# Attention with squared ReLU, then a token and channel mixer, on one Trainium2 core: a change to the planner that orders all its work

## The chip, the cores and the metric

The kernel runs on one core of one Trainium2 chip. TensorE (PE in the profile) multiplies matrices, VectorE (DVE) and ScalarE (ACT) empty its PSUM banks and do the elementwise work, GpSimd (POOL) issues the loads, and SyncE (SP) issues transposes by DMA and the stores. The metric is the device time of one execution in microseconds (us); lower is better.

## The reference

Eight batches, twelve heads, 448 positions, 64 elements a head. The attention has no softmax: the scores go through ReLU, are squared and divided by the length. Its output is the input of a mixer: one pair of products along the positions (tokens), one along the 768 channels.

```python
scores = scale * np.matmul(q, k.transpose(0, 1, 3, 2))
attn = np.maximum(scores, 0.0) ** 2 / S
x = np.matmul(attn, v)                      # then (B, S, H * D)
h = np.maximum(x.T @ w_tok1, 0.0) @ w_tok2  # 448 -> 256 -> 448, per batch
u = x + h.T
h2 = np.maximum(u @ w_ch1, 0.0) @ w_ch2     # 768 -> 1536 -> 768
out = u + h2
```

## The kernel before

The work is cut into 24 steps of four heads (three steps a batch). All products are in bf16. The names below are those of the planner's operations.

A step `s` begins with the loads of its k, q and v, issued by POOL in a fixed order (`ld`, line 386), into one of four buffers each. For k and q the head dimension must come onto the partitions. Up to step 7 this is done on PE (`T`, line 518), and ACT and DVE copy the result from PSUM (`cp`). From step 8 on it is done by DMA: DVE copies k, then q, into the tile `side` (`ik`, `iq`, line 592), and SP issues a DMA transpose from `side` into the tile `kqT` (`xk`, `xq`, line 599). There is one `side` tile, with a half for k and a half for q, so a copy of step s has to wait for the transpose of step s-1:

```python
Op(f"i{t}{s}", "DVE", emit, loads[s, t] + [cross.get((s - 1, t))], durs={"DVE": 0.534}, slack=9.0, rank=IRANK)
```

The scores come in seven chunks a step (`S`, lines 628 and 648, tiles of 64x64 rows and columns of PE, four at a time). Each chunk fills two PSUM banks; ACT or DVE apply the ReLU into a buffer `sq` (lines 363 and 365), DVE squares it (line 690). There are 13 such buffers. The product with v (`V`, lines 712 and 739) takes the seven chunks; ACT and DVE bring its two banks into the tile `xT` (`xe`).

Then the tokens are mixed: `xT` is transposed on PE (`X`, line 827) or, from step 9 on, by a DMA on SP (`xd`, line 806); `t1` and `t2` (lines 857 and 887) are the two products, and DVE adds their result to x (`u`, line 901) into the tile `uT_sb`. Of that tile SP makes a transposed copy by DMA (`ub`, line 927), which only the last addition of the kernel needs.

The channels are mixed once a batch (three steps) is there: 12 units `C1` of six matmuls (line 949, needing the weight tile `wc1`), and for each 128 rows two units `C2` of 12 matmuls (line 1022, needing the weight tile `wc2`). Each unit fills a PSUM bank. The evictions of C2 (`c2e`, line 1038) are on DVE; they add the transposed copy of u and so wait for `ub`. The stores go out through SP. `wc1` is loaded in two halves and `wc2` in three thirds, between the loads of the steps.

All of this is ordered when the kernel is built, by a class `Planner`. It walks through the time in steps of 0.01 us with a planned duration for each operation, picks the next operation for each engine, and writes the instructions in that order. On the chip each engine and each queue then works through its list in order, waiting on semaphores, whatever the planned times were. How long a DMA is planned to take follows from constants: its `work`, the share of the engines that it gets while both queues are busy (`SHARE`), a time behind it (`POST`) and a safety margin (`LATE`, `QLATE` for `kqT`, `XLATE` for `xd`, `ULATE` for `ub`). A larger margin puts the users of the data further back in the order; it does not hold anything on the chip.

Two more things stand in the kernel before. `hold`: the `ub` transposes of the first `HOLD` = 1 step get a wait for the last half of `wc1`, and since SP works in order the ones behind them wait too. And idle matmuls (`fill`, line 1100): where PE has had nothing to do for over 0.1 us of planned time, between 4.55 and 16 us, the planner writes small products of a zero tile whose result nobody reads.

Of the kernel before, what the change touches and what calls it, by code (L numbers as in the profile page):

```python
# [9 lines left out]
FP32 = mybir.dt.float32  # L10
BF16 = mybir.dt.bfloat16
# [10 lines left out]
FRONT, LOOKP, LOOKV = 40.0, 0.0, 0.0  # L22
# [16 lines left out]
class Op:  # L39
    def __init__(self, name, eng, emit, deps=(), **kw):  # L40
        self.name, self.eng, self.emit = name, eng, emit
        self.deps = [d for d in deps if d is not None]
        self.on = None
        self.start = self.seen = None
        self.banks = 0
        self.bank = []
        self.frees = None
        self.rank = 0
        self.shape = None
        self.work = None  # L50
        self.durs = None
        self.late = None
        self.drain = self.adds = 0.0
        self.slack = 0.3
        self.away = 100
        self.__dict__.update(kw)

    def ready(self, t):
        return self.left == 0 and self.at <= t


class Planner:
# [10 lines left out]
    def done(self, o):  # L73
        for d in o.users:
            d.left -= 1
            d.at = max(d.at, o.seen)
            if d.left == 0:
                self.open[d.pool].append(d)

    def moved(self, t, step):  # L80
        heads = [q for q in self.rings.values() if q and q[0][0] <= t]
        share = SHARE_W if heads and heads[0][0][2].name[:2] == "wc" else SHARE
        for q in heads:
            q[0][1] -= step * (1.0 if len(heads) == 1 else share if q[0][2].eng == "SP" else 1.0 - share)
            if q[0][1] <= 0:
                _, _, o = q.pop(0)
                o.seen = t + POST[o.eng]
                self.landed[o.eng].append(o.seen)
                o.seen += LATE[o.eng] if o.late is None else o.late
                self.done(o)  # L90

    def run(self, stream, gap, enter, tol, lanes=8):
# [28 lines left out]
        while left:  # L121
# [23 lines left out]
            for e in ("ACT", "DVE"):  # L145
# [13 lines left out]
                o = best[1]  # L159
                if t < FRONT and o.rank >= 2 and any(  # L160
                    u.rank <= 1 and u.eng == e and u.at < t + LOOKV * o.durs[e] for u in self.open["FLEX"]
                ):
                    continue
                self.open["FLEX"].remove(o)
# [11 lines left out]
            if free["PE"] <= t:  # L176
# [5 lines left out]

                def urgent(u):
                    return u.rank <= 1 if u.shape == "m" else u.name[:2] in ("V0", "V1", "V2")

                pick = None
# [10 lines left out]
                ends = late and sc.head and pick is not None  # L197
                if late and va is not None and va.first is None and va.step > (vstep if shape == "s" and sc.head else sc.vstep):
                    va = None
# [22 lines left out]
                else:  # L222
# [16 lines left out]
                    else:  # L239
                        o = pick  # L240
                if t < FRONT and LOOKP and o is not None and not urgent(o):
                    soon = [u for u in self.open["UNIT"] if u.rank <= 1] + ([va] if va is not None and urgent(va) else [])
                    soon = [u for u in soon if u.left == 0 and sum(b <= u.at for b in banks) >= u.banks]
                    now = [u for u in soon if fits(u)]
                    if now:
                        o = min(now, key=lambda u: (u.rank, u.n))
                    elif any(u.at < t + LOOKP * o.dur for u in soon):
                        o = None
# [44 lines left out]
def kernel(  # L293
# [47 lines left out]
    kqT = [[t[:, h] for t in kqTs] for h in range(2)]  # L341
    side = sbuf.tile([128, 2, KC, 128], BF16, name="side")
    q_first = side.rearrange("p a c d -> p (a c d)").bitcast(FP32).rearrange("p (e n) -> p e n", e=2)
    v_first = sbuf.tile([128, 4, 4 * D], BF16, name="v_first")
    sqs = [sbuf.tile([128, 2, S], BF16, name=f"sq{i}") for i in range(NSQ)]
# [241 lines left out]
    def crossing(s):  # L587
        for j, t in enumerate("kq"):

            def emit(o, j=j, t=t):  # L590
                src = raws[t][s % NR].rearrange("p e (c d) -> p c e d", c=KC)
                nc.vector.tensor_copy(side[:, j].rearrange("p c (e d) -> p c e d", e=2), src)

            i = raw_last[s, t] = add(
                Op(f"i{t}{s}", "DVE", emit, loads[s, t] + [cross.get((s - 1, t))], durs={"DVE": 0.534}, slack=9.0, rank=IRANK)
            )

            def emit(o, j=j):
                nc.sync.dma_start_transpose(
                    out=kqTs[s % NQ][:, j].rearrange("p (c n) -> p c n", c=KC),  # L600
                    in_=side[:, j].rearrange("p c n -> p (c n)"),
                )
# [18 lines left out]
    def score(s, c):  # L621
# [61 lines left out]
        if (s, c) == (1, SPLIT):  # L683
# [9 lines left out]
                slack=9.0,  # L693
                rank=2.1,
            )
# [3 lines left out]
    def value(s):  # L699
# [50 lines left out]
        for cs in parts:  # L750
# [13 lines left out]
            if s == 0:  # L764
                firsts.append(u)
            vals.update({s * KC + c: u for c in cs})
        raw_last[s, "v"] = u
# [28 lines left out]
    def mixing(s):  # L796
# [124 lines left out]

        hold = [wc1_ops[EC - 1]] if s < HOLD else []
        for a in range(2):
# [68 lines left out]
    def channel2(bb, t):  # L992
# [22 lines left out]
        for i, (g0, g1) in enumerate(parts):  # L1015
            cols = slice(g0 * 128, g1 * 128)
            size = (g1 - g0) * 128

            def emit(o, cols=cols, size=size):
                o.ps = bank(o, 0, "m2_ps")  # L1020
                for e in range(EC):
                    nc.tensor.matmul(  # L1022
# [119 lines left out]
```

## Time and profile before

| | |
|---|---|
| median of 3 runs | 367.15 us (364.5, 367.15, 369.16) |
| the profiled execution | 362.89 us, of which the span is 361.1 us |
| PE busy | 353.0 us (98%) |
| DVE busy | 247.7 us (69%) |
| ACT busy | 187.7 us (52%) |
| DMA packets | 98313, 50.32 MB |
| DMA transposes | 48 of `uT_sb`, 32 of `side`, 15 of `xT` |

The span runs from the first to the last instruction; the execution's own time has 1.8 us around it. A busy PE is not a PE at its peak: matmuls are pipelined and a record's length covers the pipe, so the pace is read from the starts of consecutive ones. The profiled execution is below all three runs.

### The profile page before, as it was taken

How to read it: one execution, taken by the hardware profiler on the slowest of the kernel's cores; microseconds unless marked ns; L12 is line 12 of the kernel's file. 1: busy time of each engine (PE TensorE's matmuls, PEld its weight loads, DVE VectorE, ACT ScalarE, POOL GpSimd, SP SyncE). 2: the span in 40 equal slices, each digit the busy share in tenths (PEclk: the TensorE clock that was granted, in tenths of full speed). 3: DMA queues.
4: the chain of work that ended last, by engine and by line, in shares of the span. 5: the costliest groups of instructions: out<-in, count | busy, mean ns of one | idle time of the engine just before them, and what ended most of it. 6: DMA issues, size and time to landing. Idle time of an engine off the chain costs nothing.

```text
span 361.1 us, 8783 instructions
## 1 busy us (share of the span) xinstructions
PE 353.0 (98%) x3487; PEld 200.1 (55%) x3487; DVE 247.7 (69%) x464; ACT 187.7 (52%) x388; POOL 91.1 (25%) x156
## 2 busy tenths in 40 slices
PE   8899999999899999999999999999999999999995
PEld 4556546555455554565555665556555665555564
DVE  3999598957699775998699978748699832011032
ACT  4999576637688256643674543652487212413300
POOL 8944414713323131233033321301000000000000
PEclk9999999999999999999999999999999999999999
DMA  8999999999989999999999999996621554011044
GB/s 146 187 206 200 181 183 172 190 158 204 120 122 183 213 157 147 184 120 195 185 113 145 183 147 227 140 167 120 152 40 33 95 116 120 13 45 44 0 109 112
DMA packets 98313, 50.32 MB, mean 139 GB/s; under 512 B 71968, under 2 KB 94816, under 8 KB 98272
## 3 DMA queue, kind: packets, MB, share of 16 engines
q1 hardware_dynamic: 73504, 28.16, 45.0%
q0 software_dynamic: 24608, 21.51, 44.5%
q8 instruction: 27, 0.44, 0.5%
q10 hardware_dynamic: 160, 0.10, 0.1%
q14 instruction: 14, 0.11, 0.1%
HBM read 43.45 MB, written 11.01 MB: 151 GB/s over the span
## 4 chain that ended last, share of the span: by engine, by line
PE 81%; DMA 6%; ACT 4%; issue 4%; DVE 2%; POOL 1%; ACTq 0%; POOLq 0%; DVEq 0%
PE m_ps L1022 28%; PE m_ps L949 26%; PE sc_ps L648 7%; PE acc_ps L739 7%; PE t_ps L857 5%; DMA q_raw<-in_q_dram 5%; PE h_ps L887 4%; ACT sq L363 3%; DMA k_raw<-in_k_dram 2%; DVE sq L690 1%; PE warm_ps L448 1%; DVE sq L365 1%; PE x_ps L827 1%; PE kqT_ps L518 1%; ACT kqT L369 1%
## 5 line engine op out<-in xcount | busy, mean ns | idle before, releaser
L363 ACT ACTIVATE sq<-sc_ps 128x448 bf16<-128x448 f32 x226 | 109.2, 583 | 38.6 <-PE sc_ps L648 37.8
L949 PE MATMUL m_ps<-uT_sb,wc 128*128 128x448 bf16 x576 | 115.4, 353 | 0.1
L1022 PE MATMUL m_ps<-wc,r_sb 128*128 128x384 bf16 (+2 forms) x684 | 114.1, 323 | 0.0
L690 DVE TENSOR_TENSOR sq<-sq 128x896 bf16<-128x896 bf16 x168 | 96.8, 616 | 1.0
L1022 PEld LDWEIGHTS <-r_sb 128*128 128x128 bf16 x684 | 65.8, 98 | 44.4 <-issue 2.7
L363 ACT ACTIVATE r_sb<-m_ps 128x448 bf16<-128x448 f32 x96 | 52.3, 546 | 68.0 <-PE m_ps L949 67.6
L949 PEld LDWEIGHTS <-wc 128*128 128x128 bf16 x576 | 55.2, 98 | 52.1 <-issue 4.1
L365 DVE TENSOR_SCALAR sq<-sc_ps 128x448 bf16<-128x448 f32 x110 | 63.5, 615 | 22.1 <-PE sc_ps L648 21.5
L1038 DVE TENSOR_TENSOR out_sb<-m_ps,u_sb 128x384 f32<-128x384 f32 (+2 forms) x57 | 31.2, 548 | 68.7 <-PE m_ps L1022 68.6
L386 POOL DMA_DIRECT2D v_raw<-in_v_dram x46 | 27.7, 615 | 127.9 <-PE sc_ps L648 89.0
L648 PE MATMUL sc_ps<-kqT 64*64 64x448 bf16 x644 | 50.2, 356 | 2.5 <-DVE sq L365 1.6
L739 PE MATMUL acc_ps<-sq,v_raw 64*64 64x448 bf16 x644 | 40.1, 350 | 0.0
L386 POOL DMA_DIRECT2D k_raw<-in_k_dram x48 | 29.2, 622 | 16.7 <-DMA wc<-in_moe_w_ch_dram 8.7
L363 ACT ACTIVATE r_sb<-t_ps 128x512 bf16<-128x512 f32 (+1 forms) x27 | 16.0, 604 | 29.3 <-PE t_ps L857 29.3
L648 PEld LDWEIGHTS <-kqT 64*64 64x64 bf16 x644 | 18.6, 105 | 22.0 <-issue 14.8
L901 DVE TENSOR_TENSOR uT_sb<-h_ps,xT 128x448 bf16<-128x448 f32 x48 | 28.0, 615 | 2.8 <-PE h_ps L887 2.8
L386 POOL DMA_DIRECT2D q_raw<-in_q_dram x46 | 28.1, 631 | 4.2 <-DVE out_sb L1038 1.6
L857 PE MATMUL t_ps<-x_sb,wt 128*128 128x256 bf16 (+1 forms) x216 | 25.1, 261 | 0.0
L739 PEld LDWEIGHTS <-v_raw 64*64 64x64 bf16 x644 | 18.8, 107 | 11.2 <-issue 1.6
L887 PE MATMUL h_ps<-wt,r_sb 128*128 128x448 bf16 x96 | 23.0, 354 | 0.1
L857 PEld LDWEIGHTS <-wt 128*128 128x128 bf16 x216 | 18.3, 98 | 7.0 <-issue 3.9
L772 ACT ACTIVATE xT<-acc_ps 128x448 bf16<-128x448 f32 x24 | 13.8, 573 | 12.6 <-PE acc_ps L739 12.5
(39 smaller groups left out, 118.3 us busy)
## 6 DMA issues: line engine op xcount, KB each, us to landing
out_dram<-out_sb SPq DMA_DIRECT2D x54, 192.0 KB, 3.0
k_raw<-in_k_dram POOLq DMA_DIRECT2D x48, 112.0 KB, 5.7
q_raw<-in_q_dram POOLq DMA_DIRECT2D x46, 112.0 KB, 6.9
v_raw<-in_v_dram POOLq DMA_DIRECT2D x46, 112.0 KB, 4.6
wc<-in_moe_w_ch_dram POOLq DMA_DIRECT2D x2, 1152.0 KB, 12.9
wc<-in_moe_w_ch_dram POOLq DMA_DIRECT2D x3, 768.0 KB, 14.7
u_sb<-uT_sb SPq DMA_TRANSPOSE x48, 5.4
kqT<-side SPq DMA_TRANSPOSE x32, 6.3
```

Source lines behind the costliest of these rows:

```text
L363: o.ins = nc.scalar.activation(out, ps, AF.Relu)
L365: o.ins = nc.vector.tensor_scalar(out=out, in0=ps, scalar1=0.0, scalar2=None, op0=ALU.max)
L386: nc.gpsimd.dma_start(out=raws[t][s % NR][64 * half : 64 * (half + 1)], in_=src[b, h0 : h0 + 2].rearrange("e (p c) d -> p e (c d)", c=KC),)
L648: nc.tensor.matmul(o.ps[e][64 * half : 64 * (half + 1), :S], lhsT=lhsT, rhs=rhs, start=True, stop=True, skip_group_check=True,)
L690: lambda o: nc.vector.tensor_tensor(out=buf, in0=buf, in1=buf, op=ALU.mult),
L739: nc.tensor.matmul(o.ps[half][64 * e : 64 * (e + 1), :S], lhsT=r[rows, e, c * D : (c + 1) * D], rhs=sq[rows, e, :], start=(c == 0), stop=( ...
L857: nc.tensor.matmul(o.ps[:, j, :], lhsT=wt1[:, c, j * 128 : (j + 1) * 128], rhs=x_sb[:, p0:p1, c, :], start=(c == 0), stop=(c == 3),)
L887: nc.tensor.matmul(o.ps[:, :S], lhsT=r1[:, j, a * 128 : (a + 1) * 128], rhs=wt2[:, j, :], start=(j == 0), stop=(j == JC - 1),)
L901: nc.vector.tensor_tensor(out=uTs[bb % 2][:, 2 * i + a, off : off + S].rearrange("n (c p) -> n c p", c=KC), in0=t2.ps[:, :S].rearrange("n ...
L949: nc.tensor.matmul(ps[:, :S], lhsT=wc1[:, g, e * 128 : (e + 1) * 128], rhs=uT[:, g, off : off + S], start=(g == 0), stop=(g == CC - 1),)
L1022: nc.tensor.matmul(o.ps[:, :size], lhsT=r2[:, e, t * 128 : (t + 1) * 128], rhs=wc2[:, e, cols], start=(e == 0), stop=(e == EC - 1),)
L1038: nc.vector.tensor_tensor(out=out_sb[:, cols].rearrange("n (g d) -> n g d", d=128), in0=u.ps[:, :size].rearrange("n (g d) -> n g d", d=128 ...
```

## The change

The planner's constants for DMAs change, and two are new: `SPEED` = 0.88 lets all transfers progress more slowly in the planned time, and `REST` = 2.0 puts the DVE copies into `side` 2 us (planned) behind their loads. The margins of `kqT` and `xd` transposes shrink, that of `ub` grows.

There are two `side` tiles, used in turn, and a copy of step s waits for the transpose of step s-2. (The tile that takes the first v is now a view of the second one.)

A score chunk is not placed on PE until the product with v that frees its `sq` buffer has been placed. Evictions and squares of older steps go first (`AGE`).

The first three `C2` units are divided: eight matmuls that need the first two thirds of `wc2`, and four that need the last.

`HOLD` becomes 4, and the wait is for the last third of `wc2` instead of the last half of `wc1`.

Idle matmuls are written at once wherever PE has nothing ready from 4.55 to 11 us of planned time, with a planned duration of 0.08 us before 8 us. There are 53 instead of 43.

A part of the planner that its constants had switched off is removed (left out below).

```diff
-GAP, ENTER, TOL, TPOS = 6.0, 0.5, 0.1, 3
+GAP, ENTER, TOL, TPOS = 6.0, 0.5, 0.15, 3
-QLATE, XLATE, ULATE = 4.0, 6.0, 0.5
-SHARE, SHARE_W = 0.35, 0.11
+REST, SPEED = 2.0, 0.88
+QLATE, XLATE, ULATE = 2.0, 3.0, 3.0
+SHARE, SHARE_W = 0.35, 0.2
-EARLY, PARTIAL = 3, 3
-LATE = {"POOL": 1.5, "SP": 1.0}
+DENSE, COLD = (4.55, 11.0), 8.0
+EARLY, PARTIAL, PARTIAL2 = 3, 3, 3
+LATE = {"POOL": 0.7, "SP": 1.0}
-HOLD = 1
+HOLD = 4
+AGE = 0.03
-ONE, GAP1, WAIT1, NEED1, VSOON, IRANK = 12, 12.0, 0.3, 5, 0.8, 2.0
-STOCK, SLOPE, FGAP = 10.0, 0.4, 0.5
+ONE, GAP1, WAIT1, NEED1, VSOON, IRANK = 12, 12.0, 0.2, 5, 0.8, 2.0
+STOCK, SLOPE, FGAP = 8.0, 0.5, 0.8
...
     def ready(self, t):
-        return self.left == 0 and self.at <= t
+        return self.left == 0 and self.at <= t and (self.old is None or self.old.start is not None)
...
             if d.left == 0:
+                d.at += d.rest
                 self.open[d.pool].append(d)
...
     def moved(self, t, step):
+        step = step * SPEED
...
-                if o is None and 4.55 < t < FILL and idle > 0.1:
+                quiet = o is None and DENSE[0] < t < FILL and (t < DENSE[1] or idle > 0.1)
+                if quiet:
...
-                        d = 0.056
+                        d = 0.08 if t < COLD else 0.056
...
-    side = sbuf.tile([128, 2, KC, 128], BF16, name="side")
+    sides = [sbuf.tile([128, 2, KC, 128], BF16, name=f"side{i}") for i in range(2)]
...
-                Op(f"i{t}{s}", "DVE", emit, loads[s, t] + [cross.get((s - 1, t))], durs={"DVE": 0.534}, slack=9.0, rank=IRANK)
+                Op(f"i{t}{s}", "DVE", emit, loads[s, t] + [cross.get((s - 2, t))], durs={"DVE": 0.534}, slack=9.0, rank=IRANK, rest=REST)
...
         sc[s, c] = u
+        u.old = vals.get(s * KC + c - NSQ)
...
-                    rank=2.05 if (s, c) != (1, SPLIT) else 1,
+                    rank=(2.05 if (s, c) != (1, SPLIT) else 2.0) + AGE * min(s, 4),
...
-        hold = [wc1_ops[EC - 1]] if s < HOLD else []
+        hold = [wc2_ops[EC - 1]] if s < HOLD else []
...
-            deps = [c1e[2 * bb + h, e] for h in range(2) if (t <= HT if h == 0 else t >= HT) for e in range(EC)]
-            deps += list(wc2_ops.values())
-            u = Op(f"C2.{bb}.{t}.{i}", "PE", emit, deps, shape="m", banks=1, dur=12 * (size / 2400 + 0.0025), rank=2)
+            def needs(es):
+                hs = [h for h in range(2) if (t <= HT if h == 0 else t >= HT)]
+                return [c1e[2 * bb + h, e] for h in hs for e in es] + [wc2_ops[e] for e in es]
+
+            if n * 2 + i < PARTIAL2:
+                es = range(2 * EC // 3)
+                first = Op(f"C2.{bb}.{t}.{i}a", "PE", lambda o, es=es, emit=emit: emit(o, es), needs(es), shape="m", banks=1, dur=len(es) * one, rank=2)
...
+                es = range(2 * EC // 3, EC)
+                u = Op(
+                    f"C2.{bb}.{t}.{i}",
+                    "PE",
+                    lambda o, es=es, first=first, emit=emit: emit(o, es, first),
+                    needs(es) + [first],
...
+            else:
+                es = range(EC)
+                u = Op(f"C2.{bb}.{t}.{i}", "PE", lambda o, es=es, emit=emit: emit(o, es), needs(es), shape="m", banks=1, dur=EC * one, rank=2)
```

More of the change, by code (lines that the diff above doesn't have):

```diff
@@ L197, in run @@
                 ends = late and sc.head and pick is not None
-                if late and va is not None and va.first is None and va.step > (vstep if shape == "s" and sc.head else sc.vstep):
+                stuck = sc is not None and sc.old is not None and sc.old.start is None
+                if late and not stuck and va is not None and va.first is None and va.step > (vstep if shape == "s" and sc.head else sc.vstep):
                     va = None
@@ L240, in run @@
                         o = pick
[L241 to L248, printed above, removed]
-                if o is None and 4.55 < t < FILL and idle > 0.1:
+                quiet = o is None and DENSE[0] < t < FILL and (t < DENSE[1] or idle > 0.1)
+                if quiet:
                     if filling is None:
@@ L600, in emit @@
                     out=kqTs[s % NQ][:, j].rearrange("p (c n) -> p c n", c=KC),
[L601 removed]
+                    in_=sides[s % 2][:, j].rearrange("p c n -> p (c n)"),
                 )
@@ L693, in score @@
                 slack=9.0,
-                rank=2.1,
+                rank=2.1 + AGE * min(s, 4),
             )
@@ L765, in value @@
                 firsts.append(u)
-            vals.update({s * KC + c: u for c in cs})
+            vals.update({s * KC + c: u for c in (cs if s else range(KC))})
         raw_last[s, "v"] = u
@@ L1017, in channel2, with emit @@
             size = (g1 - g0) * 128
-            def emit(o, cols=cols, size=size):
-                o.ps = bank(o, 0, "m2_ps")
-                for e in range(EC):
+            def emit(o, es, first=None, cols=cols, size=size):
+                if first is None:
+                    o.ps = bank(o, 0, "m2_ps")
+                else:
+                    o.ps, o.bank = first.ps, first.bank
+                for e in es:
                     nc.tensor.matmul(
```

24 lines of the change are left out of this document (13 added, 11 removed).

## The prediction

> **What bounds the kernel now.** I read the page first, then busy time by stages of 10 us, then the timelines of PE and DVE where a stage shows a gap. The page:
>
> ```profile
> span 361.1 us, 8783 instructions
> PE 353.0 (98%) x3487; PEld 200.1 (55%) x3487; DVE 247.7 (69%) x464; ACT 187.7 (52%) x388; POOL 91.1 (25%) x156
> DMA  8999999999989999999999999996621554011044
> ```
>
> PE is busy 98% of the span, and the DMA engines are full until about 260 us. By stages (PE first, then PEld, DVE, ACT, POOL, each with its count):
>
> ```profile
> 0.00:10.00 10.00, 8.49 (x108) 4.77 (x108) 4.13 (x13) 5.31 (x10) 8.88 (x20) 1.00 0.89 149
> 10.00:20.00 10.00, 8.93 (x211) 5.43 (x207) 9.90 (x19) 9.96 (x22) 9.31 (x16) 1.00 1.25 190
> 20.00:30.00 10.00, 9.88 (x188) 6.55 (x190) 9.87 (x20) 10.00 (x26) 4.45 (x8) 1.00 1.20 206
> ...
> 90.00:100.00 10.00, 8.37 (x82) 4.35 (x81) 6.53 (x13) 6.75 (x15) 3.56 (x6) 1.00 1.25 125
> ...
> 350.00:360.00 10.00, 7.41 (x58) 4.96 (x56) 2.57 (x6) 0.00 (x0) 0.00 (x0) 1.00 0.47 119
> sum 360.00, PE 352.96 PEld 200.07 DVE 247.68 ACT 187.70 POOL 91.14; mean PE 9.80 PEld 5.56 DVE 6.88 ACT 5.21 POOL 2.53
> ```
>
> Of 360 us PE is idle 7.04: 2.70 before 30 us, 1.63 between 90 and 100, 2.59 behind the last product, and 0.12 elsewhere. So this kernel is bound by PE from 30 us on; before that by ACT and DVE, which are both full from 10 to 30 us. In this execution, then, a better order has one hole to win, and something at the start. Here is the hole, on PE and on DVE:
>
> ```profile
> 95.33 0.54 PE L648 MATMUL sc_ps<-kqT 64*64 64x448 bf16 x5
> 97.50 0.38 PE L648 MATMUL sc_ps<-kqT 64*64 64x448 bf16 x3 [1.63 <-DVE sq L365]
> 97.81 1.31 PE L949 MATMUL m_ps<-uT_sb,wc 128*128 128x448 bf16 x6
> ```
>
> ```profile
> 91.24 1.68 DVE L690 TENSOR_TENSOR sq<-sq 128x896 bf16<-128x896 bf16 x3
> 96.30 0.62 DVE L592 COPY side<-k_raw 128x896 bf16<-128x896 bf16 x1 [3.37 <-DMA q_raw<-in_q_dram]
> 96.83 0.61 DVE L365 TENSOR_SCALAR sq<-sc_ps 128x448 bf16<-128x448 f32 x1
> ```
>
> DVE stands still for 3.37 us in front of the copy of k into `side`; the eviction behind it (L365) is what PE waits for. The profile names a load of q, but a copy of k reads no q. By the code it waits for its own k and for the DMA transpose of the step before, which reads the one `side` tile that the copy overwrites. That transpose:
>
> ```profile
> L599 SPq DMA_TRANSPOSE kqT<-side x1: 2440/2440/2440, 84.1 to 84.1; - x1
> DMA to landing us min/median/max: 12.0/12.0/12.0
> ```
>
> 84.1 + 12.0 = 96.1, and the copy starts at 96.30. So I take the reuse of `side` as the cause.
>
> Other runs of this kernel took 364.5, 367.15 and 369.16 us; the profiled one took 362.89 (span 361.1 and 1.8 around it). 1.6 to 6.3 us are lost in runs that no trace shows. What the trace shows is how little lies between some landings and their use:
>
> ```profile
> L386 POOL DMA_DIRECT2D q_raw<-in_q_dram x1: 600/600/600, 42.6 to 42.6; - x1
> DMA to landing us min/median/max: 18.3/18.3/18.3
> ...
> L435 POOL DMA_DIRECT2D wc<-in_moe_w_ch_dram x1: 760/760/760, 38.8 to 38.8; - x1
> DMA to landing us min/median/max: 18.0/18.0/18.0
> ...
> L386 POOL DMA_DIRECT2D q_raw<-in_q_dram x1: 590/590/590, 58.5 to 58.5; - x1
> DMA to landing us min/median/max: 6.4/6.4/6.4
> ```
>
> ```profile
> 60.00 1.52 PE L739 MATMUL acc_ps<-sq,v_raw 64*64 64x448 bf16 x28
> 61.35 0.39 PE L518 MATMUL kqT_ps<-ident,k_raw 64*64 64x64 bf16 x28
> ...
> 65.84 0.41 PE L518 MATMUL kqT_ps<-ident,k_raw 64*64 64x64 bf16 x28
> ...
> 57.71 0.31 PE sc_ps L648 x4
> 58.02 2.06 PE m_ps L1022 x12
> ```
>
> The q of step 6 lands at 60.9 and its transposes (T6) start at 61.35: 0.5 us in hand. The last third of `wc2` lands at 56.8 and C2.0.0.0 starts at 58.02: 1.2 us. The q of step 7 lands at 64.9 for T7 at 65.84: 0.9 us. Where transfers take a tenth longer, each of the first two is 1.8 us later and PE, which takes its work in order, waits.
>
> **The change part by part.** The work on PE stays: the same products, the same 118 changes between 64x64 and 128x128 tiles in both orders, the divided products have their 12 matmuls as 8 and 4. The prices that I move work with, from the chain that ended last:
>
> ```profile
> 295.36 5.85 PE m_ps L1022 x36
> 301.21 0.87 PE t_ps L857 x8
> ...
> 303.98 13.62 PE m_ps L949 x72
> ```
>
> So a C2 unit (12 matmuls) is 5.85/3 = 1.95 us, a C1 unit (6) is 13.62/12 = 1.14, a t1 0.87.
>
> *Two side tiles.* The k copy now waits for the transpose of two steps before. The 2.0 us go: without the wait the C1 at 97.81 would start about 95.8, one score's 0.4 behind 95.33. DVE's other waits of this kind,
>
> ```profile
> DVE side L592 <- DMA kqT<-side: 3.0, 2, 1.7
> ```
>
> held no matmul, and are worth nothing on PE. Bounds 1.6 (the gap shown) to 2.1; I take 2.0.
>
> *Longer transfers in the plan* (SPEED, REST, QLATE, XLATE, LATE). This only moves work. In the changed order, T6 has two thirds of C2.0.0.1 and t1.4.0 more in front, and V5 (60.00 to 61.35) and S5.6 (0.31) less: 1.30 + 0.87 - 1.35 - 0.31 = half a us more in hand. T7 has 5 C2 and 9 C1 units more in front: 9.8 + 10.3 us. Up to V8 (the products with v of step 8), 14 C2 units are done instead of 6, so step 8 comes 15.6 us later against its loads. Worth 0 in an execution without lateness; in the others up to the 4.3 us between the profiled execution and the median. Price if it fails: the margin taken off the x transposes (XLATE 6 to 3) leaves t1 waiting, about a us each for the few that now land closest. I take 0 for the profiled execution.
>
> *Divided C2.* C2.0.0.0 starts with 8 matmuls that need two thirds of `wc2`; the last third is needed 1.30 + 0.87 us later (t1.4.0 stands between), so its margin grows from 1.2 to about 3 us. 0 us in the profiled execution.
>
> *Late channel-input transposes.* The eight transposes of steps 0 to 3 now wait for the last third of `wc2`, and the four of steps 4 and 5 stand behind them on SP's queue. Before, the two of step 0 waited for the last half of `wc1`, and eleven went from 29.80 on:
>
> ```profile
> 29.80 39.93 SPq L927 DMA_TRANSPOSE u_sb<-uT_sb  x11
> ...
> L927 SPq DMA_TRANSPOSE u_sb<-uT_sb x2: 1711/2598/3484, 45.7 to 49.3; - x2
> DMA to landing us min/median/max: 14.5/15.2/15.8
> ...
> L927 SPq DMA_TRANSPOSE u_sb<-uT_sb x3: 1189/1220/1464, 65.3 to 68.5; - x3
> DMA to landing us min/median/max: 6.4/6.5/9.8
> ```
>
> Behind them on SP stand the transposes of step 8 and the stores. Waiting for them: the evictions of C2 on DVE, behind those the u additions of step 5 and the copies into `side`; and six C2 units keep six of eight PSUM banks until then. Counting rows from C2.0.0.0a at 57.7, the sixth C2 unit ends near 76, and with two banks for t2.5 PE stops there if the third transpose has not landed. At 1.22 us an issue it is issued by 56.8 + 2 x 1.22 = 59.2 and lands between 65.7 (6.5 later) and 75.0 (15.8 later). Cost 0 at that pace, with 1 us in hand at the worst; the gain is on the loads from 30 to 57 us, which held no matmul here. I take 0.
>
> [...]
>
> *Idle matmuls.* 53 instead of 43, in the first step:
>
> ```profile
> 4.58 0.63 PE L1100 MATMUL fill_ps<-warm 128*128 128x128 bf16 x4
> ...
> 6.25 0.94 PE L1100 MATMUL fill_ps<-warm 128*128 128x128 bf16 x10
> ...
> 11.46 0.84 PE L1100 MATMUL fill_ps<-warm 128*128 128x128 bf16 x12
> ```
>
> Ten more are 10 x 0.07 to 10 x 0.16 us of PE, in stretches where PE has nothing ready and ACT and DVE set the pace (up to V0 both engines have the same number of instructions in both orders). The four at 4.58 take twice the time each of the twelve at 11.46, so early work on PE is slow; denser work might end that sooner. Bounds: 1.6 lost to 1.1 won (half of the 2.2 us from 4.58 to 6.8). I take 0.
>
> *Sum.* 362.89 - 2.0 = 360.9 us for an execution like the profiled one. For the median of runs I add nothing for lateness, since each margin of under 1.2 us found here grows; bounds 0 to 4.3. Forecast 361.0, 6 us under the median of before.
>
> **The rivals.**
> *Faster still, near 359.3.* Early PE work gets to full speed sooner (1.1) and 0.5 of the 2.70 us that PE idles before 30 us goes: 360.9 - 1.6. For it: the slow idle matmuls. Against it: ACT and DVE are full from 10 to 30 us. [...]
> *The lost time of the other runs is not lateness.* Then 4.3 us stay on top: 360.9 + 4.3 = 365.2. For it: all three runs lie above the profiled one. Against it: margins of 0.5 to 1.2 us behind landings of 18 us.
> *Slower, 370.* SP issues the held transposes at the 3.5 us that one took at 45 to 49 us, and they land after 15.8: the sixth is issued at 56.8 + 5 x 3.5 = 74.3 and lands at 90; the second group of C2 evictions, in front of the squares of step 6 on DVE, is due near 81 (76 and four C1 units): 9 us of PE, 361 + 9 = 370. It decides from 6 us on; with a second such round (the loads of steps 7 to 9 pushed back) over 374.5. Against it: landings behind the weights took 6.4 to 9.8.
>
> **How the numbers follow.** Forecast 361.0 (own range 359.8 to 363): 0.40. Faster, 359.3: 0.32. Lost time stays: 0.12. Slower: 0.16, of which 0.04 within 2%. 2% of 367.15 is 7.3 us, about what a measurement of this kernel can tell from no change; under 359.8 is faster, over 374.5 slower. So faster 0.32, within 2% 0.56, slower 0.12. The range 358.3 to 368.0 leaves out most of the slower rival and a little below.
>
> **What would show it.** Right: no gap on PE at the k copies, T7 over 15 us behind its loads, a span near 359.2, idle of PE under 0.5 us from 30 to 350. Wrong: a PE gap between 70 and 95 us ended by an output eviction or a u addition on DVE; t1 waiting for x transposes; idle matmuls followed by a later V0 than before.

## The result and the profile after

The changed kernel takes 360.81 us (median of 6 runs, 360.34 to 360.97). The kernel before, run beside it, was at 364.5 us (median of four runs, 362.6 to 367.15). The ratio is 0.989, with a 95% interval of 0.985 to 0.994: a gain of about one per cent, clear of noise. The forecast was 361.0. Executions over 1.5% above the fastest of the same kernel are left out of every median and ratio here (two of six of the kernel before, 2 to 6 of the 17 to 31 that ran beside the experiments, and those that the table shows).

The profiled execution took 360.45 us. The page after, the rows that answer to the three shown first of before:

```profile
span 358.7 us, 8814 instructions
PE 351.2 (98%) x3497; PEld 199.0 (55%) x3497; DVE 245.5 (68%) x462; ACT 190.7 (53%) x390; POOL 91.1 (25%) x156
DMA  8999999996999999999989999997532244121044
```

The share of PE is the same 98%, so the page alone shows only a shorter span. The stages show where PE is idle (stretch, its length, then PE, PEld, DVE, ACT and POOL busy with their counts, granted clock, DMA share, GB/s):

```profile
0.00:30.00 30.00, 26.33 (x515) 16.16 (x519) 24.32 (x51) 25.38 (x54) 21.15 (x39) 1.00 1.10 174
30.00:90.00 60.00, 60.00 (x723) 33.35 (x716) 41.59 (x77) 34.78 (x71) 22.43 (x37) 1.00 1.23 180
90.00:100.00 10.00, 10.00 (x107) 5.85 (x106) 7.17 (x14) 7.51 (x16) 3.55 (x6) 1.00 0.95 124
100.00:350.00 250.00, 249.88 (x2123) 140.13 (x2121) 170.60 (x318) 122.98 (x253) 43.99 (x74) 1.00 0.84 129
```

From 30 to 350 us PE is idle for 0.12 us. Before 30 us it is idle for 3.67 us, against 2.70 in the kernel before, so no idle time was won there. The stage from 90 to 100, which had 1.63 us of idle time, has none. On DVE's timeline the copies into `side` in that stage carry no wait any more (start, length, operation, and in brackets the idle time before it with its releaser):

```profile
91.30 0.62 DVE L357 TENSOR_SCALAR sq<-sc_ps 128x448 bf16<-128x448 f32 x1 [1.44 <-PE sc_ps L640]
91.85 0.61 DVE L584 COPY side<-k_raw 128x896 bf16<-128x896 bf16 x1
...
93.44 0.61 DVE L584 COPY side<-q_raw 128x896 bf16<-128x896 bf16 x1
```

The one wait of DVE here is for scores from PE, the engine that sets the end. Between landings and uses there is now this much (three starts on PE, then issue and landing of the last third of `wc2`, of the q loads of step 6, and of the channel-input transposes that now start with the last third of `wc2`):

```profile
57.06 1.46 PE L1018 MATMUL m_ps<-wc,r_sb 128*128 128x384 bf16 x8
...
59.23 2.11 PE L1018 MATMUL m_ps<-wc,r_sb 128*128 128x384 bf16 x12
61.27 0.41 PE L510 MATMUL kqT_ps<-ident,k_raw 64*64 64x64 bf16 x28
...
86.38 0.41 PE L510 MATMUL kqT_ps<-ident,k_raw 64*64 64x64 bf16 x28
...
L427 POOL DMA_DIRECT2D wc<-in_moe_w_ch_dram x2: 750/755/760, 39.0 to 39.8; - x2
DMA to landing us min/median/max: 10.6/12.2/13.7
...
L378 POOL DMA_DIRECT2D q_raw<-in_q_dram x2: 647/652/656, 41.7 to 42.3; - x2
DMA to landing us min/median/max: 13.5/13.5/13.5
...
L920 SPq DMA_TRANSPOSE u_sb<-uT_sb x11: 1217/1262/2522, 53.5 to 73.9; - x11
DMA to landing us min/median/max: 5.9/8.0/11.2
```

The last third of `wc2` is issued at 39.8, lands by 39.8 + 13.7 = 53.5, and the first matmuls that need it are in the group at 59.23: 5.7 us in hand, where there were 1.2. The q of step 6 lands at 42.3 + 13.5 = 55.8 for T6 at 61.27: 5 us, where there was half a us. T7 starts at 86.38 instead of 65.84, and its loads of k and q had been issued before 56. The transposes on SP start at 53.5, when the last third of `wc2` has landed, instead of 29.8.

### The profile page after: what moved, and what is told of

It reads as the page before. It is cut to its first block, busy times and chain, and to the rows that moved or that the text cites. A ratio compares the mean times of both kernels' runs of the same rounds, so it can differ in the third digit from the quotient of the medians.

```text
span 358.7 us, 8814 instructions
## 1 busy us (share of the span) xinstructions
PE 351.2 (98%) x3497; PEld 199.0 (55%) x3497; DVE 245.5 (68%) x462; ACT 190.7 (53%) x390; POOL 91.1 (25%) x156
## 4 chain that ended last, share of the span: by engine, by line
PE 92%; ACT 4%; DMA 1%; DVE 1%; issue 1%; SPq 0%; ACTq 0%; DVEq 0%
PE m_ps L942 31%; PE m_ps L1018 31%; PE sc_ps L640 9%; PE acc_ps L732 8%; PE t_ps L850 6%; PE h_ps L880 5%; ACT sq L355 3%; DMA side<-in_q_dram 1%; PE x_ps L820 1%; PE kqT_ps L510 1%; DVE sq L683 1%; ACT kqT L361 0%; ACT x_sb L361 0%; SPq L450 0%; ACT q_raw L361 0%
## 5 line engine op out<-in xcount | busy, mean ns | idle before, releaser
L355 ACT ACTIVATE sq<-sc_ps 128x448 bf16<-128x448 f32 x226 | 108.1, 567 | 34.0 <-PE sc_ps L640 33.9
L357 DVE TENSOR_SCALAR sq<-sc_ps 128x448 bf16<-128x448 f32 x110 | 64.5, 616 | 24.5 <-PE sc_ps L640 24.4
L1054 DVE TENSOR_TENSOR out_sb<-m_ps,u_sb 128x384 f32<-128x384 f32 (+2 forms) x57 | 30.9, 546 | 52.7 <-PE m_ps L1018 52.7
L640 PE MATMUL sc_ps<-kqT 64*64 64x448 bf16 x644 | 49.2, 356 | 0.3
L880 PE MATMUL h_ps<-wt,r_sb 128*128 128x448 bf16 x96 | 22.2, 354 | 0.0
L767 DVE TENSOR_SCALAR xT<-acc_ps 128x448 bf16<-128x448 f32 x24 | 14.8, 616 | 2.5 <-PE acc_ps L732 2.5
```

What stands on the lines that cost most here:

```text
L355: o.ins = nc.scalar.activation(out, ps, AF.Relu)
L357: o.ins = nc.vector.tensor_scalar(out=out, in0=ps, scalar1=0.0, scalar2=None, op0=ALU.max)
L640: nc.tensor.matmul(o.ps[e][64 * half : 64 * (half + 1), :S], lhsT=lhsT, rhs=rhs, start=True, stop=True, skip_group_check=True,)
L880: nc.tensor.matmul(o.ps[:, :S], lhsT=r1[:, j, a * 128 : (a + 1) * 128], rhs=wt2[:, j, :], start=(j == 0), stop=(j == JC - 1),)
L1054: nc.vector.tensor_tensor(out=out_sb[:, cols].rearrange("n (g d) -> n g d", d=128), in0=u.ps[:, :size].rearrange("n (g d) -> n g d", d=128 ...
```

## The experiments

Kernels called "before + ..." put one part of the change into the old kernel; kernels called "after, ..." take one part out of the new one. The planner makes a new order each time, so each shows a part together with the order that it leads to. Each kernel ran on the same chip as the kernel before, which gives its ratio:

| kernel | median us (lowest to highest), runs that count | before on that chip | ratio, 95% interval |
|---|---|---|---|
| before + two side tiles | 368.27 (365.77 to 370.81), 6 | 362.78 | 1.017 [1.014, 1.021] |
| before + longer transfers | 365.53 (364.99 to 365.98), 4 | 362.78 | 1.008 [1.005, 1.011] |
| after, one side tile | 362.84 (361.82 to 365.51), 10 | 362.78 | 1.001 [0.998, 1.004] |
| after, old transfer times | 371.12 (368.81 to 372.39), 4 | 362.78 | 1.023 [1.019, 1.027] |
| after, again | 361.16 (360.46 to 362.10), 10 | 363.33 | 0.994 [0.991, 0.998] |
| before + two side tiles + 6 us behind loads | 363.52 (361.89 to 366.79), 7 of 10 | 363.33 | 1.003 [0.999, 1.006] |
| before + two side tiles + longer transfers | 364.36 (363.21 to 367.88), 7 of 9 | 363.33 | 1.006 [1.002, 1.010] |
| after, old hold | 363.26 (362.31 to 363.55), 10 | 363.33 | 1.001 [0.998, 1.003] |
| before, again | 363.97 (362.84 to 368.13), 8 | 364.22 | 1.004 [0.999, 1.010] |
| after, no rest behind loads | 360.98 (360.02 to 365.27), 10 | 364.22 | 0.992 [0.988, 0.996] |
| after, C2 whole | 361.29 (360.25 to 361.98), 10 | 364.22 | 0.993 [0.989, 0.997] |
| after, no idle matmuls | 362.05 (360.82 to 364.24), 10 | 364.22 | 0.995 [0.991, 0.999] |

### Two side tiles alone

```diff
-    side = sbuf.tile([128, 2, KC, 128], BF16, name="side")
+    sides = [sbuf.tile([128, 2, KC, 128], BF16, name=f"side{i}") for i in range(2)]
...
-                Op(f"i{t}{s}", "DVE", emit, loads[s, t] + [cross.get((s - 1, t))], ...
+                Op(f"i{t}{s}", "DVE", emit, loads[s, t] + [cross.get((s - 2, t))], ...
...
```

> The kernel before with two side tiles used in turn, and nothing else of the change (the same 43 idle matmuls, and the same 27 C1 and 6 C2 units in front of V8). If the hole of 2.0 us was the reuse of side (my theory): DVE no longer stands still in front of a k copy near 96 us, the profiled execution takes about 361 us, the median falls by about 2 us, and the spread of the runs stays some 4 to 6 us, since the margins of T6, T7 and wc2 are as before. If it was the load of q, as the profile names it: the gap of about 1.6 us on PE stays. If side was behind the spread as well: the runs come within 1 us of each other, near 361.

It lost 5.5 us. The traced execution is the shortest of the six (365.77 us, its span 2.9 us longer than that of the kernel before), so it shows a part of the loss. In it the stage of the hole has only 0.71 us of PE idle left, but a new one stands at 194. DVE's timeline, PE's timeline, the q loads concerned, and the row of DVE's waits that sums these up (us in total, times, longest):

```profile
194.50 0.62 DVE L592 COPY side<-q_raw 128x896 bf16<-128x896 bf16 x1 [2.40 <-issue]
```

```profile
193.02 0.37 PE L648 MATMUL sc_ps<-kqT 64*64 64x448 bf16 x1
195.71 0.57 PE L648 MATMUL sc_ps<-kqT 64*64 64x448 bf16 x7 [2.32 <-DVE sq L365]
```

```profile
L386 POOL DMA_DIRECT2D q_raw<-in_q_dram x2: 647/652/656, 182.5 to 183.1; - x2
...
DMA to landing us min/median/max: 9.0/10.1/11.3
```

```profile
DVE side L592 <- issue: 8.6, 5, 3.4
```

The profile names no releaser for the copy ("issue"), but the second q load, issued at 183.1, landed 11.3 us later, at 194.4, and the copy starts at 194.50. With two tiles the planner is free to put the copy right behind the planned landing of its load. The load is late, DVE stands still in order, the eviction behind it is late, and PE waits 2.32 us. In the kernel before, by this reading, the wait for the one tile had put these copies later in the order: it was a lost wait in one place and a margin in the others. A kernel with two tiles and later copies, further below, tests this.

### The longer transfers alone

```diff
-QLATE, XLATE, ULATE = 4.0, 6.0, 0.5
-SHARE, SHARE_W = 0.35, 0.11
+REST, SPEED = 2.0, 0.88
+QLATE, XLATE, ULATE = 2.0, 3.0, 3.0
+SHARE, SHARE_W = 0.35, 0.2
...
-LATE = {"POOL": 1.5, "SP": 1.0}
+LATE = {"POOL": 0.7, "SP": 1.0}
...
```

> The kernel before with only the planner's constants for DMAs changed (SPEED, REST, SHARE_W, QLATE, XLATE, ULATE, LATE); one side tile, hold on wc1 for step 0, whole C2. In the order T7 has 4 C1 and 5 C2 units more in front (about 14 us). If late landings cost the runs their 4 us (my theory): the spread falls to about 1 us and the median to 361 to 362. If the lost time of the runs is no lateness: the median stays within 1 us of that of before. If side is what matters: a gap at the k copies again and 364 to 366.

It lost 2.75 us (the traced spans differ by 2.3). On PE:

```profile
59.57 1.12 PE L743 MATMUL acc_ps<-sq,v_raw 64*64 64x448 bf16 x20
61.37 0.38 PE L743 MATMUL acc_ps<-sq,v_raw 64*64 64x448 bf16 x4 [0.68 <-DVE sq L694]
61.91 0.38 PE L743 MATMUL acc_ps<-sq,v_raw 64*64 64x448 bf16 x4 [0.15 <-DVE sq L694]
62.92 0.62 PE L831 MATMUL x_ps<-ident,xT 128*128 128x128 bf16 x8 [0.63 <-ACT xT L776]
```

These are not late transfers but work placed too early. As the plan now expects `wc2` later, C2 stands behind the product with v of step 5, which runs into its own squares: three gaps of 1.46 us together. The rest of the loss was not followed. The hole at the k copies is gone here too, with one side tile: PE is busy for all of 90 to 100 us. So longer transfers in the plan cost nothing only where other ready work can take the place, which the whole change provides and this kernel does not.

### The same two parts taken out of the new kernel

```diff
-    sides = [sbuf.tile([128, 2, KC, 128], BF16, name=f"side{i}") for i in range(2)]
+    sides = [sbuf.tile([128, 2, KC, 128], BF16, name=f"side{i}") for i in range(1)]
...
-                Op(f"i{t}{s}", "DVE", emit, loads[s, t] + [cross.get((s - 2, t))], ... rest=REST)
+                Op(f"i{t}{s}", "DVE", emit, loads[s, t] + [cross.get((s - 1, t))], ... rest=REST)
...
```

> The changed kernel with one side tile (a copy waits for the transpose of the step before; the first v has a tile of its own). 126 changes of tile shape instead of 118, 8 x 0.11 = 0.9 us. If the plan with longer transfers is what matters (my theory): 361 to 362.5, no hole, spread under 1 us, since the plan knows of the wait. If the second side tile is what matters: 363 or more and a spread of several us.

Its ratio of 1.001 [0.998, 1.004] lies above that of the whole change on another chip, 0.994 [0.991, 0.998], so the second tile is worth about 0.6% there, some 2 us. But there is no hole at the k copies in its trace. Its span is 2.7 us longer than the first of the changed kernel (361.4 against 358.7). Its one PE wait over 0.3 us behind 30 us is 0.7 us, of a `t1` for an x transpose by DMA. About 0.9 more would be the eight further changes of tile shape (126 in its trace, 118 in the changed kernel), at the 0.11 us each that the expectation took; it is an estimate from the kernel before, where a C2 unit next to 64x64 work takes 2.06 us (at 58.02) and one among 128x128 work 1.95 (at 292.65). What the last us consists of was not settled.

```diff
-REST, SPEED = 2.0, 0.88
-QLATE, XLATE, ULATE = 2.0, 3.0, 3.0
-SHARE, SHARE_W = 0.35, 0.2
+REST, SPEED = 0.0, 1.0
+QLATE, XLATE, ULATE = 4.0, 6.0, 0.5
+SHARE, SHARE_W = 0.35, 0.11
...
-LATE = {"POOL": 0.7, "SP": 1.0}
+LATE = {"POOL": 1.5, "SP": 1.0}
```

> The changed kernel with the old constants for DMAs (SPEED 1, REST 0, SHARE_W 0.11, QLATE 4, XLATE 6, ULATE 0.5, LATE 1.5); two side tiles, the hold on wc2 and the divided C2 stay. No C2 unit stands in front of T7 (9 in the changed kernel). If late landings matter: T7, the output evictions or the C2 units wait by some us, 362 to 366, and the runs spread by 3 us or more. If the side tiles and the hold are all that matters: 361, spread under 1 us.

With the old transfer times the new kernel takes 371.12 us, 2.3% more than before. PE is idle for 8.9 us between 30 and 350. The largest of its gaps, on PE and on DVE, and the k loads behind it:

```profile
113.76 1.49 PE L640 MATMUL sc_ps<-kqT 64*64 64x448 bf16 x8 [3.65 <-DVE out_sb L1054]
```

```profile
112.63 0.62 DVE L584 COPY side<-k_raw 128x896 bf16<-128x896 bf16 x1 [5.19 <-issue]
```

```profile
L378 POOL DMA_DIRECT2D k_raw<-in_k_dram x2: 622/628/635, 101.4 to 102.0; - x2
...
DMA to landing us min/median/max: 8.1/9.3/10.6
```

PE's wait is put down to an output eviction (L1054), which looks like the rival with the held transposes. DVE's timeline says otherwise. The eviction stood behind a k copy that had waited 5.19 us, and the load of that k landed at 102.0 + 10.6 = 112.6. For this gap it is the same mechanism as with two side tiles alone. The next largest, 1.57 us at 91.96, is put down to a transpose out of `side`; the others were not followed. So in the order that two tiles allow, the new constants for transfers are worth ten us: 371.1 against 361.

### Is it the early copies, or more?

With the two tiles as above:

```diff
+REST = 6.0
...
+                d.at += d.rest
...
-                Op(f"i{t}{s}", ... [cross.get((s - 1, t))], ... rank=IRANK)
+                Op(f"i{t}{s}", ... [cross.get((s - 2, t))], ... rank=IRANK, rest=REST)
```

> The kernel before with two side tiles, and the copies into side put 6 us (planned) behind the landing of their loads (REST = 6); nothing else. If the second side tile alone was slower because the copies came to stand on DVE right behind loads that land late (my theory now): the waits of DVE in front of the copies and the 2.3 us gap on PE go, and the time falls from 368 to 361 to 363. If the second tile is slower because its transposes start earlier and slow the loads: still 366 or more.

Putting the copies 6 us behind their loads takes the 5.5 us back: 363.52, no different from before. So the loss of the two tiles was the early copies, but no gain is left. In the trace DVE waits for no load in front of a copy into `side`. That execution is a long one for another reason (367.35 us): PE waits 3.2 us once in front of a `t1` for an x transpose by DMA.

The kernel before with both parts, two side tiles and the longer transfers (their two diffs in one):

> The kernel before with two side tiles and the planner's new constants for DMAs (REST = 2 among them); hold on wc1 for step 0, whole C2. With the margins alone PE lost 2.0 us near V5, where the plan had nothing to do while it waited for wc2 and the order had C2 behind. If the hold and the divided C2 are needed against that (my theory): the 2 us near 60 stay and it takes 363 to 365, behind the changed kernel. If tiles and margins are all that matters: 360.5 to 361.5.

364.36 us, 0.6% slower than before. Its trace has the same three gaps at the product with v of step 5 (0.68, 0.15 and 0.63 us), and no hole at the k copies. The two parts that the prediction counted on do not make the gain by themselves.

```diff
-HOLD = 4
+HOLD = 1
...
-        hold = [wc2_ops[EC - 1]] if s < HOLD else []
+        hold = [wc1_ops[EC - 1]] if s < HOLD else []
```

> The changed kernel with the channel-input transposes held as before (step 0, until the last half of wc1). If the hold matters through the weights: wc2 lands later again (about 57 instead of 53.5 us) and k and q of step 6 too, and with the plan for longer transfers PE has a gap of 1 us or more before 70: 362 to 364. [...]

363.26 against 361.16 for the whole change on the same chip, and the two sets of ten runs do not overlap. The landing of the three thirds of `wc2`, first with the old hold, then in the first execution of the changed kernel, and the places on PE where the old hold loses time:

```profile
L427 POOL DMA_DIRECT2D wc<-in_moe_w_ch_dram x3: 740/750/850, 33.4 to 40.4; - x3
...
DMA to landing us min/median/max: 15.9/16.8/20.4
```

```profile
L427 POOL DMA_DIRECT2D wc<-in_moe_w_ch_dram x3: 750/760/803, 33.8 to 39.8; - x3
...
DMA to landing us min/median/max: 10.6/12.2/13.7
```

```profile
36.46 1.18 PE L880 MATMUL h_ps<-wt,r_sb 128*128 128x448 bf16 x4
37.58 0.97 PE L640 MATMUL sc_ps<-kqT 64*64 64x448 bf16 x8
...
58.77 0.38 PE L640 MATMUL sc_ps<-kqT 64*64 64x448 bf16 x4
59.97 1.03 PE L850 MATMUL t_ps<-x_sb,wt 128*128 128x256 bf16 x8 [0.82 <-DVE x_sb L363]
```

With the transposes out of the way each third lands 4 to 7 us earlier. With the old hold, the plan puts a `t1` in front of the first C2, and PE waits 0.82 us for its input. So the late transposes are worth 2 us here, of which this gap shows 0.8. The first product with v started at the same time as in the profile of the whole change beside it (15.94 and 15.99), so the rest lies behind it too. Some of it shows in the length of the rows at 36.46 and 37.58: the same work takes 0.93 and 0.57 us in the whole change (at 34.76 and 36.38 of its first profile), so 0.65 us more here. At that time no `wc2` was due, so this is only the other order.

### Lateness, and what did not matter

The kernel before once more, for the profile of another execution:

> The kernel before once more, for the trace of another of its executions. If its runs above the quiet ones lose their time to late landings (my theory): a span over 361.1 us has PE gaps that a load or a DMA transpose ends, at T6, C2.0.0.0, T7, t1 or the copies into side, which add up to what the span has more; a span at or under 361.1 has one or none. If the lost time is no lateness: the PE gaps are as in the first trace and the span is longer all the same.

```profile
57.73 1.47 PE L1022 MATMUL m_ps<-wc,r_sb 128*128 128x384 bf16 x8
60.98 0.81 PE L1022 MATMUL m_ps<-wc,r_sb 128*128 128x384 bf16 x4 [1.78 <-DMA wc<-in_moe_w_ch_dram]
...
63.76 0.41 PE L518 MATMUL kqT_ps<-ident,q_raw 64*64 64x64 bf16 x26 [0.25 <-DMA q_raw<-in_q_dram]
```

```profile
96.55 0.62 DVE L592 COPY side<-k_raw 128x896 bf16<-128x896 bf16 x1 [1.50 <-DMA kqT<-side]
```

The same instructions lose 1.78 us at `wc2` and 0.25 at the q of step 6, the two places named in the prediction. The last third of `wc2` was issued 2.9 us later than in the first trace (41.7 against 38.8) and landed 19.3 us after its issue instead of 18.0, so most of its lateness lay before its issue. The hole at 96 is gone: since PE is 2 us later, the tile is free when the k copy is due, but for 1.50 us that no matmul feels. That wait is now put down to the transpose out of `side`, not to a q load. So in this order one loss can stand in for the other: with PE held at `wc2`, the tile costs nothing.

The changed kernel once more, for a comparison on the chip of the old hold:

> The changed kernel once more, so that its parts are compared on one chip. 360.3 to 361.0 as in its first runs, whatever the kernel before takes on this chip. If its time followed the chip as that of before does: 358 to 363.

0.994 [0.991, 0.998], 2.2 us faster there; the interval overlaps that of the first comparison. The profiled execution has a span of 359.8, 1.1 more than the first one, and PE's timeline shows where it begins (four idle matmuls and the first product with v, in the first execution and in this one):

```profile
4.28 0.39 PE L1116 MATMUL fill_ps<-warm 128*128 128x128 bf16 x4
...
14.99 0.95 PE L705 MATMUL acc_ps<-sq,side 64*64 64x448 bf16 x16
```

```profile
4.58 0.63 PE L1116 MATMUL fill_ps<-warm 128*128 128x128 bf16 x4
...
15.99 0.38 PE L705 MATMUL acc_ps<-sq,side 64*64 64x448 bf16 x4
```

The same instructions ran at two paces, and the first product with v came 1.0 us later. Between 30 and 350 us both executions leave PE idle for 0.12 us.

```diff
-REST, SPEED = 2.0, 0.88
+REST, SPEED = 0.0, 0.88
```

> The changed kernel with REST = 0: the copies into side are planned right at their loads' landing. If REST is what makes the second side tile safe (my theory): DVE waits several us in all in front of the copies, PE in one or two places 1 us or more behind it, 362 to 365 with a spread of 2 us or more. If SPEED and the other margins are enough: 360.5 to 361.5 and a spread under 1.5 us.

360.98: no PE wait over 0.3 us behind 30 us, and the same time. DVE stands 3.7 us in front of one copy into `side`, and no matmul feels it. The 2 us of rest behind the loads are not what protects the new order. One run in ten took 365.27, and whether the rest keeps such runs away ten runs don't tell.

```diff
-EARLY, PARTIAL, PARTIAL2 = 3, 3, 3
+EARLY, PARTIAL, PARTIAL2 = 3, 3, 0
```

> The changed kernel without divided C2 units (PARTIAL2 = 0). wc2 landed at 53.5 us in the changed kernel and its last third was needed at 59.2, so on the chip the division covers nothing; by that 360.8 to 361.5. But the planner believes in a later landing and puts 3 C2 in front of T7 instead of 9: if that order lacks work near 60 us, PE has a gap of 1 to 2 us there and it takes 362 to 363.

361.29, with a range (360.25 to 361.98) like that of the whole change run again. The division is worth nothing that can be measured.

```diff
-FILL = 16.0
+FILL = 0.0
```

> The changed kernel without any idle matmuls after the first eight long ones (FILL = 0; the 53 are left out, no other work moves). If they keep PE at full pace in the first 16 us: the transposes and scores there take about twice as long each (0.11 us for 128 columns), but ACT and DVE set the pace, so 361 to 362.5. If PE's pace does not hang on them: 360.8 to 361.2. If PE's slow pace reaches the first products of the mixer: 363 or more.

362.05 (the 53 idle matmuls are left out): perhaps one us more than the three other versions near 361, with ranges that overlap. Two stages of the first step and the second part of the first product with v, all without idle matmuls, then the first part of that product in the kernel before:

```profile
12.00:14.00 2.00, 1.91 (x16) 0.53 (x12) 2.00 (x5) 2.00 (x6) 1.96 (x4) 0.61 1.27 185
14.00:16.00 2.00, 2.00 (x34) 1.16 (x34) 2.00 (x5) 2.00 (x6) 1.63 (x3) 0.54 1.18 160
```

```profile
18.01 0.76 PE L705 MATMUL acc_ps<-sq,side 64*64 64x448 bf16 x12 [1.26 <-ACT sq L355]
```

```profile
15.24 0.95 PE L712 MATMUL acc_ps<-sq,v_first 64*64 64x448 bf16 x16
```

Without them the granted clock falls to about half (0.61 and 0.54, where the changed kernel has 1.00) between 12 and 16 us, yet the second part of that product, at 18.01, waits 1.26 us for ACT. The first profile of the changed kernel has the same wait of 1.3 us. So there ACT is the last to be ready with idle matmuls and without, and it hides what the slow matmuls cost: 18.01 is 0.17 us later than in that first profile. The start in the kernel before, 15.24, lies between the two of the changed kernel (14.99 and 15.99): more idle matmuls did not bring the first product forward.

The traced execution without idle matmuls has a span 1.9 us longer than that first one (360.6 against 358.7), and loses most of it at a late load. DVE waits for it once, in front of the copy of q at 185.24, and PE behind that:

```profile
DVE side L584 <- DMA q_raw<-in_q_dram: 2.6, 1, 2.6
```

```profile
186.45 0.38 PE L640 MATMUL sc_ps<-kqT 64*64 64x448 bf16 x4 [1.21 <-DVE sq L357]
```

The order is the same in both. Scores in front of this place start 0.18 us later than in the first execution (183.72 against 183.54), the `t1` behind it 1.73 us later (187.86 against 186.13). So the changed order, too, can be caught by a late load at a copy into `side`, and the us in the median is not shown to be the price of the idle matmuls.

## Why the prediction was right or wrong

**The bound and the time: right.** PE set the end before and sets it now. Span 358.7 (359.2 was forecast), no gap at the k copies, 0.12 us of PE idle from 30 to 350, T7 20 us later: each named sign of being right is there. One sign of being wrong came as well, in the second profile of the changed kernel: a first product with v later than before (15.99 against 15.24). Of the 2.4 us between the profiled spans the hole is 1.6 to 2.0 by the prediction's own rows. The first product with v came 0.25 us earlier (14.99 against 15.24), but in the second profile of the kernel before it came at 14.95, so that is scatter. The gain was forecast less well than the time: 6 us under the median of before, where 3.7 were measured (364.5 to 360.8).

**Two side tiles, 2.0 us: the cause right, the price not separable.** That the reuse of `side` held the copy is borne out by the execution in which the profile itself names the transpose. But the step took the wait away in thought and left all else in place. In the kernel the planner used the freedom to put the copies early, and the tiles alone cost 5.5 us; with the copies put back, nothing was gained. Nor is the second tile needed for the hole to go: with one tile it is gone in the kernel with the longer transfers alone and in the new kernel with one side tile.

**Longer transfers, 0 in the profiled execution: wrong as a term by itself.** Alone they cost 2.75 us, as C2 moved behind work that was not ready; taken out of the whole change they were worth ten. The price that I named if they failed (`t1` waiting for x transposes made by DMA) came in neither; the new kernel with one side tile had one such wait, of 0.7 us. The sum came out right because what these parts lose alone and what others gain cancelled in the whole. I read it so: the longer times give the margin that the one tile had given, and the hold gives the other early work its data. The prediction had not counted on this; it is luck that its terms of 0 added up.

**What no run separates.** The rule for score chunks, `AGE` and five more constants (`TOL`, `WAIT1`, `STOCK`, `SLOPE`, `FGAP`) were neither put in alone nor taken out, and the prediction gave them no term. On one chip, the kernel before with both main parts took 364.36 us and the changed kernel with the old hold 363.26; they differ by these, the divided C2 and the idle matmuls. So these parts may be worth about a us, and that the three main parts are enough is not shown.

**Up to 4.3 us of lateness: the mechanism right, the size too large.** The kernel before, traced again, lost 2.03 us at just the two thin margins named, and the changed kernel with its margins of 5 us and more there varies by 0.6 to 1.6 us where before varies by over 4. But the 4.3 was the distance to a median of three runs of 364.5 to 369.16; to the later medians (362.8 to 364.5) it is 0 to 1.6. Of the longest executions of before no trace was had, so that they lose time in the same places stays open. Their granted clock on record points to gaps on PE: of the 67 executions of before that count beside the experiments, the eight with a mean clock of 0.995 or lower took 364.2 to 366.5 us, and the other 59 have a median of 363.0. In the traces a mean clock of 0.994 and 0.991 went with PE gaps of 3.65 and 3.2 us (the old transfer times, the two tiles with 6 us of rest); but without idle matmuls 0.995 came from the first 16 us, so this points to gaps and does not prove them. The rival "lost time is not lateness" did not come true in the execution that was traced.

**Late channel-input transposes, 0: too low.** They are worth 2 us. I had priced only the cost of the delay and had seen that no load between 30 and 57 us held a matmul in the trace. What I left out is that the plan makes another order when the transposes are out of the way: `wc2`, landing 4 to 7 us earlier, is used earlier (the first C2 starts at 58.23 instead of 60.84). The feared wait for the held transposes did not come: they were issued at 1.2 to 2.5 us each and landed after 5.9 to 11.2, where the slower rival needed 3.5 and 15.8. Nor did the second round at the loads of steps 7 to 9: from 30 to 350 us PE is idle for 0.12 us. Whether the delay removes DMA time or only moves it is not settled: in the four stages of 10 us from 30 to 70 us the DMA share is 1.20, 1.16, 1.34 and 1.36, against 1.21, 1.28, 1.30 and 1.32 with the old hold (5.06 against 5.11 in sum). The thirds of `wc2` do go faster without the transposes beside them (10.6 to 13.7 us to landing, against 15.9 to 20.4). That moving paid because `wc2` was due first is my reading; the gap of 0.82 us is what the rows show of it.

**Divided C2, 0: right. Idle matmuls, 0: not settled to better than a us.** The four idle matmuls at the start took 0.39 us in the first profile after and 0.63 before, which looks like the faster rival. But the second profile of the changed kernel has 0.63 too, with a span 1.1 longer. Five traced executions run the same first step (the changed kernel twice, without rest, with C2 whole, with the old hold). Their first product with v starts at 14.99, 15.99, 15.21, 14.84 and 15.94 us, and the four idle matmuls at the start take 0.39, 0.63, 0.60, 0.39 and 0.63 us. So the 1.1 us that this rival put on an early full pace are about what the pace can cost, but they come and go from run to run with the same instructions; they are not a gain of the change.

## What to carry to other kernels

In an order that each engine works through strictly, a wait that looks like a pure loss can be the margin that covers another lateness. Before taking it away, list what will move forward into the space and how late its data can be. Read the time between each landing and its use, not only the gaps of one execution, and test a part both alone and taken out of the whole: here neither of the two main parts pays alone, nor both together, nor the whole change without the later transposes.

## What was not expected of the hardware

A gap on PE cost more than its length. In the kernel with the old transfer times, the stages around the gap of 3.65 us that ended at 113.76:

```profile
110.00:112.00 2.00, 0.12 (x4) 0.00 (x0) 0.00 (x0) 0.60 (x2) 1.59 (x3) 1.00 1.91 141
...
114.00:116.00 2.00, 2.00 (x11) 0.56 (x10) 2.00 (x5) 1.09 (x3) 0.00 (x0) 0.50 1.40 190
116.00:118.00 2.00, 2.00 (x11) 1.07 (x10) 2.00 (x5) 0.76 (x2) 0.00 (x0) 0.76 1.26 200
```

The granted clock falls to 0.50 and is not yet back at full in the stage behind 116 (0.76): eight matmuls of the scores took 1.49 us at 113.76, against 0.57 for seven behind the gap of 2.32 us at 195.71 in the kernel with two side tiles alone, where the granted clock is 1.00 in every stage from 190 to 205. With two side tiles and 6 us of rest, the execution whose longest gap on PE behind the start is 3.2 us has a mean granted clock of 0.991. And without idle matmuls the clock fell to 0.54 although no gap of PE behind the start was over 0.9 us until then. So in these traces the length of one gap does not tell by itself whether the clock falls.

The same load varied with what ran beside it: a third of `wc2` landed after 10.6 to 13.7 us in the first execution of the changed kernel, where the transposes of `uT_sb` wait for it, after 15.9 to 20.4 with the old hold, and after 14.2 to 18.0 in the first trace of the kernel before.
